# Five changes to an attention and mixture-of-adapters kernel: the first batch's patch sums on TensorE, the router on GpSimd, the up-projection moved within a slot, later batches prepared in equal steps, tail copies on ScalarE

## The chip, the cores and the metric

One core of one Trainium2 chip. The metric is device time in microseconds (us), the median of several executions of the same program; lower is better. A *span* is the length of one profiled execution inside the core, about 2 us shorter than the time that is measured around it.

TensorE (PE in the profile) multiplies matrices, PEld loads its weights, VectorE is DVE, ScalarE is ACT, GpSimd is POOL, and SyncE (SP) issues transfers. PEclk is the share of TensorE's full clock that was granted; the profile shows 1.00 where its record of the clock has not begun yet, which matters below.

## The reference, cut to what matters

```python
def _attn_ref(q, kv, w_sr):                     # q (4, 12288, 128), kv (4, 384, 32, 128)
    kv_pool = kv.reshape(B, H//4, 4, W//4, 4, C).mean(axis=(2, 4))   # 4x4 patches
    k = v = kv_pool.reshape(B, -1, C) @ w_sr                         # 768 keys per batch
    a = softmax(q @ k.T / sqrt(C))                                   # written out there
    return a @ v

def _moe_ref(x, w_gate, A, B):                  # x: 49152 tokens, 8 experts of rank 16
    logits = x @ w_gate
    # the two largest logits of each token, softmax over the two -> w
    # delta = sum over the two experts of w * ((x @ A[e]) @ B[e])
    return x + delta
```

## The kernel before: the parts that matter here

The 49152 tokens are cut into 96 chunks of 512, 24 to a batch. The main loop runs one *slot* per chunk position `k`. In slot `k` TensorE computes the scores of chunk `k` in three pieces, and ScalarE takes their exponential (`em`). TensorE also attends chunk `k-4`, and VectorE normalizes chunk `k-5`. An older chunk goes through transposes, down-projection, gate and up-projection (`tts`, `h_ps`, `hg`, `d_ps`, `osb`). Every fourth slot *routes*: it computes the expert weights of four chunks at once. The last eight chunks are routed in the smaller groups 2, 2, 2, 1, 1.

```python
    def prepare(b, adder):                      # pool, project and lay out one batch's keys and values
        ...                                     # pool_step: u += v on `adder`, five steps per third of the batch
        for h in range(3):
            for step in range(5):
                if adder is nc.vector:
                    n = w = 1024 if step < 3 else 512
                else:
                    n, w = 1024 if step < 3 else 512, 512
                ...
        def keys(h):
            ...
            for i in range(2):
                mm(ps[:, i], kvr[b, h][:, 0, 0, i, 0:C], id_f, is_transpose=True, start=(i == 0), stop=(i == 1))
            keep(nc.vector.tensor_scalar(kpT[:, 2 * h:2 * h + 2], ps, 1.0 / 16.0, None, op0=ALU.mult))
        def keys2(h): ...                       # w_sr x kpT -> kfT
        def values(h):                          # three of the six blocks each, two calls
            ...
    def route(k0, step):
        ...
        if step == 0:
            keep(nc.vector.tensor_tensor(m12, so[:, :, 0], so[:, :, 1], op=ALU.add))
            keep(nc.vector.scalar_tensor_tensor(arg, lg, 2.0, m12..., op0=ALU.mult, op1=ALU.subtract))
            keep(nc.scalar.activation(th, arg, AF.Tanh, bias=0.0, scale=0.5))
            keep(nc.vector.tensor_tensor(mask, lg, so[:, :, 1]..., op=ALU.is_ge))
        else:
            keep(nc.vector.scalar_tensor_tensor(w[:, 0:n], th, 1.0, mask, op0=ALU.add, op1=ALU.mult))   # gw
    ...
    for m in range(GC):                         # the start
        turn_q(0, m, nc.scalar)                 # 16 transposes of q on TensorE
    sums, rest = prepare(0, nc.vector)
    for h in range(3):
        for item in sums[h] + rest[2 * h:2 * h + 2]:    # VectorE adds, then keys, keys2
            item()
        for k in range(LA):
            scores(k, h)
    for item in rest[6:]:                       # values
        item()
    ...
    for k in range(LA, last + 2):               # the slots
        ...                                     # 9 <= i < 21: GpSimd adds the next batch's kv, two or three a slot
        if ks: scores(k, 0)
        if kn is not None: normalize(kn)        # rinv, xn
        for x_, h_ in pairs: transposes(x_, h_) # tt_ps, then the copy tts on VectorE
        ...
        if ks: scores(k, 1)
        if ka is not None: attend(ka, 0)
        if kn is not None:
            top(kn)                             # srt
            if ends: route(first[kn], 0)
        for h_ in kh[:1]: up(h_)                # d_ps
        if ks: scores(k, 2)
        for h_ in kh[:1]: finish(h_)            # osb and the store
        if ends: route(first[kn], 1)
        for x_ in kx[:1]:
            down(x_)
            gate(x_)                            # hg = h_ps * gw
        ...                                     # the rest of attend; one or two preparation steps from i = 18 on
```

The softmax here doesn't subtract the row's maximum and nothing guards it: scores larger than these inputs give would overflow.

## Time and profile before

| what | value | where it is read |
|---|---|---|
| time | 467.4 us median (466.7 to 469.2, 4 runs) | the times |
| span of the profiled run | 462.2 us | head of the page |
| start, to chunk 1's reciprocal | 47.46 us | timeline of VectorE |
| clean slot | 3.83 us | distance of reciprocals |
| routing slot, GpSimd quiet / adding | 0.28 / 0.5 to 3.1 us more | the same |
| preparing one later batch | about 6.9 us over eight slots | the same |
| chunk 88's reciprocal to the end | 41.0 us | the same |

Each slot has exactly one VectorE reciprocal, `rinv`, so the distance between two of them is the cost of a slot. That cuts the span into three stretches: the start (to chunk 1), the loop (chunk 1 to chunk 88, 87 slots), and the tail. I use chunk 1 and not chunk 0, because the change takes chunk 0 early.

From the page of the kernel before, the busy time of two engines, the granted clock in 40 equal slices (tenths), and the chain of work that ended last:

```profile
PE 406.1 (88%) x4475; PEld 302.1 (65%) x4547; DVE 364.9 (79%) x1033; ACT 295.6 (64%) x325; POOL 97.0 (21%) x101
...
PEclk9658999999999999999999999999999999999996
...
PE 43%; DVE 31%; issue 5%; DVEq 0%
```

TensorE is the busiest engine, but VectorE holds almost a third of the chain: both decide the time. The clock that the profile shows is low in slices 2 to 4, in the start, and in the last slice.

Groups of instructions of the kernel before (line, engine, operation, result and operands, shapes, count; then busy us and the mean ns of one; then idle time before them):

```profile
L281 DVE TENSOR_TENSOR mask<-xn,srt 128x128 f32<-128x128 f32 x22 | 13.0, 592 | 0.0
...
L275 DVE SCALAR_TENSOR_TENSOR arg<-xn,m_3051 128x128 f32<-128x128 f32 x1 | 0.3, 294 | 0.0
...
L167 POOL TENSOR_TENSOR kvr<-kvr 128x512 f32<-128x512 f32 x63 | 78.7, 1272 | 183.4 <-PE tt_ps L67 57.9 <-PE sg L67 56.6 <-DMA kvr<-in_kv_dram 44.2
```

The same `arg` takes 0.29 us in this slot and 1.30 us in another (next view), and 1.30 is about the length of one GpSimd add, 1.27 us. The timeline of the kernel before shows them side by side in one routing slot (start, length in us, engine, line, operation). The first and last line are the two reciprocals that bound the loop; VectorE and GpSimd were asked for separately:

```profile
47.46 0.18 DVE L241 RECIPROCAL rinv<-acc 128x4 f32<-128x4 f32 x1 [1.91 <-PE acc L67]
...
89.33 1.30 DVE L275 SCALAR_TENSOR_TENSOR arg<-xn,m_1165 128x128 f32<-128x128 f32 x1
90.55 0.28 DVE L281 TENSOR_TENSOR mask<-xn,srt 128x128 f32<-128x128 f32 x1
...
91.36 1.05 DVE L287 SCALAR_TENSOR_TENSOR gw<-th,mask 128x128 f32<-128x128 f32 x1
...
85.52 4.97 POOL L167 TENSOR_TENSOR kvr<-kvr 128x512 f32<-128x512 f32 x4 [0.72 <-DMA kvr<-in_kv_dram]
90.42 0.53 POOL L78 DMA_DIRECT2D qbf_1451<-in_q_dram  x1
90.96 1.28 POOL L167 TENSOR_TENSOR kvr<-kvr 128x512 f32<-128x512 f32 x1
...
421.16 0.17 DVE L241 RECIPROCAL rinv<-acc 128x4 f32<-128x4 f32 x1
```

`arg` ends at 90.63 us, just behind GpSimd's run of four adds (85.52 + 4.97 = 90.49 us); `mask`, the same size, ran right after it in 0.28 us while GpSimd issued a transfer; `gw` then stretched beside the next add.

Waits of the kernel before (engine and line, what it waited for, us in total, times, longest):

```profile
PEld L67 <- DVE tts L305: 19.1, 91, 0.8
...
DVE osb L332 <- PE d_ps L67: 14.9, 67, 0.7
```

The first is a stall of some 0.2 us in nearly every slot: the up-projection's weights wait for VectorE's copy `tts`.

Busy time in stretches of the kernel before (the first line names the columns; busy us and count of instructions per engine, then the granted clock):

```profile
core 0: us, PE busy (x) PEld busy (x) DVE busy (x) ACT busy (x) POOL busy (x), PEclk, DMA share, GB/s
...
13.00:18.00 5.00, 1.85 (x4) 0.79 (x4) 2.76 (x5) 0.00 (x0) 0.00 (x0) 0.63 1.09 381
18.00:23.00 5.00, 3.83 (x9) 0.96 (x9) 4.79 (x6) 3.59 (x4) 0.00 (x0) 0.50 1.09 380
...
33.00:38.00 5.00, 3.79 (x10) 1.69 (x11) 0.46 (x2) 3.03 (x4) 0.00 (x0) 0.50 0.87 145
38.00:43.00 5.00, 4.33 (x34) 3.29 (x33) 1.43 (x4) 3.06 (x5) 0.00 (x0) 0.98 0.88 242
```

So the start ran TensorE at half clock from about 14.3 to 38 us. From 10.3 to 15.2 us TensorE was idle, waiting for VectorE's first sums.

### The profile page before, as it was taken

The numbers are of one execution on the slowest core, as the hardware profiler recorded it, in microseconds if no ns is written. First come the engines' busy times: TensorE is split into PE (matmuls) and PEld (weight loads), VectorE is DVE, ScalarE is ACT, GpSimd is POOL, SyncE is SP. The second block draws the span as 40 slices with busy tenths as digits, with TensorE's granted clock in tenths as the row PEclk, the third lists the DMA queues.
The fourth block names the chain that finished last, engine by engine and source line by source line (L and its number), as shares of the span: only waits on it lengthen the run. The fifth ranks groups of instructions, "written<-read, shape, count | busy, mean of one in ns | idle before, by whom it ended". The sixth has DMA issues, their size and how long they took to land.

```text
span 462.2 us, 11209 instructions
## 1 busy us (share of the span) xinstructions
PE 406.1 (88%) x4475; PEld 302.1 (65%) x4547; DVE 364.9 (79%) x1033; ACT 295.6 (64%) x325; POOL 97.0 (21%) x101
## 2 busy tenths in 40 slices
PE   4578998989999988979999988978999999999872
PEld 3126776766777766756777766756677777777761
DVE  2752588878688888878788888897788888888995
ACT  3338976756577667756667777755667777777300
POOL 0011734810000835720000537450000000000000
PEclk9658999999999999999999999999999999999996
DMA  8998949985237978996145899999234244422222
GB/s 279 377 221 201 214 137 216 260 184 119 71 90 196 253 215 225 254 203 142 47 115 126 251 246 230 256 194 207 70 94 115 69 115 116 109 75 70 70 92 91
DMA packets 127427, 76.42 MB, mean 165 GB/s; under 512 B 50480, under 2 KB 126512, under 8 KB 127024
## 3 DMA queue, kind: packets, MB, share of 16 engines
q1 hardware_dynamic: 126384, 64.11, 51.6%
q0 software_dynamic: 704, 11.54, 13.4%
q8 instruction: 35, 0.57, 0.5%
q14 instruction: 16, 0.13, 0.1%
q10 hardware_dynamic: 288, 0.07, 0.1%
HBM read 50.53 MB, written 36.70 MB: 189 GB/s over the span
## 4 chain that ended last, share of the span: by engine, by line
PE 43%; DVE 31%; issue 5%; DVEq 0%
PE acc L67 17%; PE sg L67 10%; DVE xn L246 8%; DVE tts L305 7%; PE d_ps L67 5%; PE h_ps L67 4%; DVE hg L319 3%; PE tt_ps L67 3%; DVE mask L281 3%; DVE gw L287 2%; DVE srt L265 1%; DVE rinv L241 1%; PE kfT_ps L67 1%; PE v_ps L67 1%; DVE kfT L198 1%
## 5 line engine op out<-in xcount | busy, mean ns | idle before, releaser
L229 ACT ACTIVATE em<-sg 128x1024 f16<-128x1024 f32 x288 | 284.2, 1021 | 120.9 <-PE sg L67 87.2
L67 PE MATMUL acc<-vx,em 128*128 128x137 f16 x2304 | 174.9, 224 | 8.3 <-DVE xn L246 5.4
L67 PEld LDWEIGHTS <-em 128*128 128x128 f16 x2304 | 150.1, 98 | 36.6 <-DVE xn L246 30.6
L67 PE MATMUL sg<-qT,kfT 128*128 128x512 bf16 x504 | 159.7, 390 | 3.9 <-ACT em L229 1.6
L167 POOL TENSOR_TENSOR kvr<-kvr 128x512 f32<-128x512 f32 x63 | 78.7, 1272 | 183.4 <-PE tt_ps L67 57.9
L67 PEld LDWEIGHTS <-tts 128*128 128x128 bf16 x768 | 51.2, 98 | 41.3 <-DVE tts L305 19.1
L332 DVE TENSOR_TENSOR osb<-d_ps,xn 128x512 f32<-128x512 f32 x96 | 66.2, 689 | 14.9 <-PE d_ps L67 14.9
L246 DVE TENSOR_TENSOR xn<-acc,rinv 128x544 f32<-128x544 f32 x96 | 69.6, 725 | 3.4
L319 DVE TENSOR_TENSOR hg<-h_ps,gw 128x512 bf16<-128x512 f32 x96 | 66.3, 691 | 2.6
L305 DVE COPY tts<-tt_ps 128x1024 bf16<-128x1024 bf16 (+1 forms) x99 | 65.9, 670 | 0.8 <-PE tt_ps L67 0.7
L67 PEld LDWEIGHTS <-kfT 128*128 128x128 bf16 x576 | 46.8, 99 | 13.6 <-issue 8.0
L67 PEld LDWEIGHTS <-xn 128*128 128x128 bf16 x384 | 29.1, 98 | 31.3 <-issue 8.8
L67 PE MATMUL tt_ps<-id_bf,xn 128*128 128x128 bf16 x384 | 37.1, 219 | 10.1 <-DVE osb L332 6.2
L67 PE MATMUL tt_ps<-id_bf,hg 128*128 128x128 bf16 x384 | 37.3, 220 | 7.6 <-DVE hg L319 7.6
L67 PE MATMUL d_ps<-b_bf,tts 128*128 128x128 bf16 x384 | 38.5, 223 | 4.3 <-DVE tts L305 1.1
L241 DVE RECIPROCAL rinv<-acc 128x4 f32<-128x4 f32 x96 | 17.2, 179 | 30.6 <-PE acc L67 30.6
L67 PE MATMUL h_ps<-a_bf,tts 128*128 128x128 bf16 x384 | 37.1, 219 | 1.2
L265 DVE MAX8 srt<-xn 128x8 f32<-128x8 f32 x384 | 34.9, 154 | 0.1
L67 PEld LDWEIGHTS <-hg 128*128 128x128 bf16 x384 | 24.9, 98 | 9.7 <-DVE hg L319 9.7
L279 ACT ACTIVATE th<-arg 128x128 f32<-128x128 f32 (+2 forms) x27 | 8.0, 298 | 30.3 <-DVE arg L275 30.0
L167 DVE TENSOR_TENSOR kvr<-kvr 128x1024 f32<-128x1024 f32 (+1 forms) x12 | 13.1, 1090 | 6.0 <-DMA kvr<-in_kv_dram 5.4
L207 DVE CAST vx<-v_ps 128x408 f16<-128x408 f32 x8 | 4.7, 584 | 12.1 <-PE v_ps L67 12.0
(112 smaller groups left out, 129.8 us busy)
## 6 DMA issues: line engine op xcount, KB each, us to landing
kvr<-in_kv_dram SPq DMA_DIRECT2D x96, 256.0 KB, 4.8
out_dram<-osb SPq DMA_DIRECT2D x96, 256.0 KB, 2.8
qf<-in_q_dram SPq DMA_DIRECT2D x4, 256.0 KB, 5.6
qbf_286<-in_q_dram POOLq DMA_DIRECT2D x1, 512.0 KB, 5.9
qbf_288<-in_q_dram POOLq DMA_DIRECT2D x1, 512.0 KB, 7.8
qbf_507<-in_q_dram POOLq DMA_DIRECT2D x1, 512.0 KB, 9.9
qbf_810<-in_q_dram POOLq DMA_DIRECT2D x1, 512.0 KB, 7.1
qbf_1127<-in_q_dram POOLq DMA_DIRECT2D x1, 512.0 KB, 6.5
```

The lines of the kernel that those rows point to most:

```text
L67: return keep(nc.tensor.matmul(*a, **k))
L167: keep(adder.tensor_tensor(u[:, lo:hi], u[:, lo:hi], v[:, lo:hi], op=ALU.add))
L229: keep(nc.scalar.activation(em[k][:, 2 * r:2 * r + 2], ps, AF.Exp, bias=0.0, scale=scale))
L241: keep(nc.vector.reciprocal(ri, acc[k][:, :, VC]))
L246: keep(nc.vector.tensor_tensor(x, acc[k][:, :, 0:VC], ri.unsqueeze(2).broadcast_to([P, S, VC]), op=ALU.mult))
L265: keep(nc.vector.max(srt[k0][:, m, s], xn[k][:, s, C:VC]))
L279: keep(nc.scalar.activation(th, arg, AF.Tanh, bias=0.0, scale=0.5))
L281: keep(nc.vector.tensor_tensor(mask, lg, so[:, :, 1].unsqueeze(2).broadcast_to([P, n, 8]), op=ALU.is_ge))
L287: keep(nc.vector.scalar_tensor_tensor(w[:, 0:n], th, 1.0, mask, op0=ALU.add, op1=ALU.mult))
L305: keep(nc.vector.tensor_copy(sb[:, lo:hi], ps[:, lo:hi]))
L319: keep(nc.vector.tensor_tensor(hg[k].rearrange("p s (e r) -> p (s e) r", e=E), hp[k].rearrange("p s (e r) -> p (s e) r", e=E), gw[k0][:, m ...
L332: keep(nc.vector.tensor_tensor(osb, dp[k], xn[k][:, :, 0:C], op=ALU.add))
```

## The change

The intent has five parts:

1. **Start.** VectorE adds only neighbouring row pairs (four adds per third of the batch). The rest of the 4x4 sum is made by 16 accumulating transposes on TensorE, where there were 2. The values of a third come right behind its scores, and chunk 0 is attended before the first slot's scores.
2. **Router on GpSimd**, with one extra slot before the gate that uses it.
3. **`up` behind the third scores** of a slot, so that it need not wait for the copy `tts`.
4. **Preparation of later batches** in three equal steps per third, with the GpSimd adds issued later in the slot.
5. **Tail:** once no scores are left, the `tts` copies go to ScalarE.

```diff
+        def pair_step(h, r, x):
+            u, v = (kvr[b, h][:, r + i, x].rearrange("p g c -> p (g c)") for i in range(2))
+            keep(adder.tensor_tensor(u, u, v, op=ALU.add))
 ...
-            for i in range(2):
-                mm(ps[:, i], kvr[b, h][:, 0, 0, i, 0:C], id_f,
-                   is_transpose=True, start=(i == 0), stop=(i == 1))
+            if adder is nc.vector:
+                parts = [(r, x, c) for r in (0, 2) for x in range(2) for c in range(2)]
+            else:
+                parts = [(0, 0, 0)]
+            for n, (r, x, c) in enumerate(parts):
+                for i in range(2):
+                    mm(ps[:, i], kvr[b, h][:, r, x, i, c * C:(c + 1) * C], id_f, is_transpose=True,
+                       start=(n == 0 and i == 0), stop=(n == len(parts) - 1 and i == 1))
 ...                                             # values: two blocks in each of three calls
-            keep(nc.vector.tensor_tensor(m12, so[:, :, 0], so[:, :, 1], op=ALU.add))
-            keep(nc.vector.scalar_tensor_tensor(arg, lg, 2.0, m12..., op0=ALU.mult, op1=ALU.subtract))
+            def over(i):                        # lg - so[i]
+                keep(nc.gpsimd.tensor_tensor(d, lg, so[:, :, i]..., op=ALU.subtract))
+            arg, mask = over(0), over(1)
+            keep(nc.gpsimd.tensor_tensor(arg, arg, mask, op=ALU.add))
             keep(nc.scalar.activation(th, arg, AF.Tanh, bias=0.0, scale=0.5))
-            keep(nc.vector.tensor_tensor(mask, lg, so[:, :, 1]..., op=ALU.is_ge))
+            keep(nc.gpsimd.tensor_scalar(mask, mask, 0.0, None, op0=ALU.is_ge))
 ...
-            keep(nc.vector.scalar_tensor_tensor(w[:, 0:n], th, 1.0, mask, op0=ALU.add, op1=ALU.mult))
+            keep(nc.gpsimd.tensor_tensor(w[:, 0:n], th, mask, op=ALU.mult))
+            keep(nc.gpsimd.tensor_tensor(w[:, 0:n], w[:, 0:n], mask, op=ALU.add))
 ...
-        keep(nc.vector.tensor_copy(sb[:, lo:hi], ps[:, lo:hi]))
+        if tail:                                # tail = not ks: no scores left
+            keep(nc.scalar.copy(sb[:, lo:hi], ps[:, lo:hi]))
+        else:
+            keep(nc.vector.tensor_copy(sb[:, lo:hi], ps[:, lo:hi]))
 ...
-        for item in sums[h] + rest[2 * h:2 * h + 2]:
+        for item in sums[h] + rest[3 * h:3 * h + 2]:
             item()
         for k in range(LA):
             scores(k, h)
-    for item in rest[6:]:
-        item()
+            if k == 1:
+                rest[3 * h + 2]()               # values of this third
 ...
-        enter.setdefault(first[k] + size[k] + LA + (k - first[k]), []).append(k)
+        e = first[k] + size[k] + LA + (k - first[k]) + (size[k] == GC)
+        enter.setdefault(e, []).append(k)
 ...                                             # GpSimd's adds: from the head of a slot to its end
+        if k == LA:
+            for s in range(S):                  # chunk 0 attended before the scores
+                attend(ka, s)
+            ka = None
 ...
-        for h_ in kh[:1]:
-            up(h_)
         if ks:
             scores(k, 2)
         for h_ in kh[:1]:
+            up(h_)
             finish(h_)
```

More of the change, by code (lines that the diff above doesn't have):

```diff
@@ L167, in pool_step @@
             keep(adder.tensor_tensor(u[:, lo:hi], u[:, lo:hi], v[:, lo:hi], op=ALU.add))
+        def pair_step(h, r, x):
+            u, v = (kvr[b, h][:, r + i, x].rearrange("p g c -> p (g c)") for i in range(2))
+            keep(adder.tensor_tensor(u, u, v, op=ALU.add))
         for h in range(3):
-            block = []
-            for step in range(5):
-                if adder is nc.vector:
-                    n = w = 1024 if step < 3 else 512
-                else:
-                    n, w = 1024 if step < 3 else 512, 512
-                for lo in range(0, n, w):
-                    block.append(lambda h=h, step=step, lo=lo, w=w: pool_step(h, step, lo, lo + w))
-            sums.append(block)
+            if adder is nc.vector:
+                sums.append([lambda h=h, r=r, x=x: pair_step(h, r, x)
+                             for r in (0, 2) for x in range(2)])
+                continue
+            sums.append([lambda h=h, step=step, lo=lo: pool_step(h, step, lo, lo + 512)
+                         for step in range(5) for lo in range(0, 1024 if step < 3 else 512, 512)])
         st = {}
@@ L187, in keys @@
             ps = mtile([P, 2, P], name="kpT_ps")
-            for i in range(2):
-                mm(ps[:, i], kvr[b, h][:, 0, 0, i, 0:C], id_f,
-                   is_transpose=True, start=(i == 0), stop=(i == 1))
+            if adder is nc.vector:
+                parts = [(r, x, c) for r in (0, 2) for x in range(2) for c in range(2)]
[5 more added lines that the diff above has]
+                       start=(n == 0 and i == 0), stop=(n == len(parts) - 1 and i == 1))
             keep(nc.vector.tensor_scalar(kpT[:, 2 * h:2 * h + 2], ps, 1.0 / 16.0, None,
@@ L203, in values @@
                 keep(nc.vector.memset(vx[b][:, :, VC:VE], 1.0))
-            ps = mtile([P, 3, VC], name="v_ps")
-            for i in range(3):
-                mm(ps[:, i], st["kpT"][:, 3 * h + i], wext, start=(i == 0), stop=(i == 2))
-            keep(nc.vector.tensor_copy(vx[b][:, 3 * h:3 * h + 3, 0:VC], ps))
+            ps = mtile([P, 2, VC], name="v_ps")
+            for i in range(2):
+                mm(ps[:, i], st["kpT"][:, 2 * h + i], wext, start=(i == 0), stop=(i == 1))
+            keep(nc.vector.tensor_copy(vx[b][:, 2 * h:2 * h + 2, 0:VC], ps))
         for h in range(3):
-            rest.append(lambda h=h: keys(h))
-            rest.append(lambda h=h: keys2(h))
-        for h in range(2):
-            rest.append(lambda h=h: values(h))
+            for f in (keys, keys2, values):
+                rest.append(lambda h=h, f=f: f(h))
         return sums, rest
@@ L271, in route @@
         if step == 0:
-            m12 = rpool.tile([P, GC * S], FP32, tag="m12", name="m12")[:, 0:n]
-            keep(nc.vector.tensor_tensor(m12, so[:, :, 0], so[:, :, 1], op=ALU.add))
-            arg = rpool.tile([P, GC * S, 8], FP32, tag="arg", name="arg")[:, 0:n]
-            keep(nc.vector.scalar_tensor_tensor(
-                arg, lg, 2.0, m12.unsqueeze(2).broadcast_to([P, n, 8]),
-                op0=ALU.mult, op1=ALU.subtract))
+            def over(i):
+                d = rpool.tile([P, GC * S, 8], FP32, tag=f"over{i}", name=f"over{i}")[:, 0:n]
+                keep(nc.gpsimd.tensor_tensor(
+                    d, lg, so[:, :, i].unsqueeze(2).broadcast_to([P, n, 8]), op=ALU.subtract))
+                return d
+            arg, mask = over(0), over(1)
+            keep(nc.gpsimd.tensor_tensor(arg, arg, mask, op=ALU.add))
             th = rpool.tile([P, GC * S, 8], FP32, tag="th", name="th")[:, 0:n]
             keep(nc.scalar.activation(th, arg, AF.Tanh, bias=0.0, scale=0.5))
-            mask = rpool.tile([P, GC * S, 8], FP32, tag="mask", name="mask")[:, 0:n]
-            keep(nc.vector.tensor_tensor(
-                mask, lg, so[:, :, 1].unsqueeze(2).broadcast_to([P, n, 8]), op=ALU.is_ge))
+            keep(nc.gpsimd.tensor_scalar(mask, mask, 0.0, None, op0=ALU.is_ge))
             rt[k0] = th, mask
@@ L286, in route, with transposes @@
             w = rpool.tile([P, GC * S, 8], FP32, tag="gw", name="gw")
-            keep(nc.vector.scalar_tensor_tensor(w[:, 0:n], th, 1.0, mask, op0=ALU.add, op1=ALU.mult))
+            keep(nc.gpsimd.tensor_tensor(w[:, 0:n], th, mask, op=ALU.mult))
+            keep(nc.gpsimd.tensor_tensor(w[:, 0:n], w[:, 0:n], mask, op=ALU.add))
             gw[k0] = w
-    def transposes(kx, kh):
+    def transposes(kx, kh, tail):
         ps = mtile([P, 2, S, P], BF16, name="tt_ps")
@@ L347 @@
             scores(k, h)
-    for item in rest[6:]:
-        item()
+            if k == 1:
+                rest[3 * h + 2]()
+    rest = []
     late = const.tile([P, 1], FP32)
@@ L387 @@
                 load_kv(b + 1, h, j, 1)
-            if 9 <= i < 21:
-                h, j = divmod(i - 9, 4)
-                for _ in range(3 if j == 3 else 2):
-                    if sums[h]:
-                        sums[h].pop(0)()
+        if k == LA:
+            for s in range(S):
+                attend(ka, s)
+            ka = None
         if ks:
@@ L399 @@
         for x_, h_ in pairs:
-            transposes(x_, h_)
+            transposes(x_, h_, not ks)
         if k + 1 in range(GC + 1, 2 * GC):
@@ L432 @@
         kh = kx
+        if b + 1 < B and 9 <= i < 21:
+            h, j = divmod(i - 9, 4)
+            for _ in range(3 if j == 3 else 2):
+                if sums[h]:
+                    sums[h].pop(0)()
         if i >= 18 and rest:
```

## The prediction

> **What bounds it now** (span 462.2 us). The timeline, by the spacing of the `rinv` reciprocals (one a slot):
> - Clean slots take 3.83 us, TensorE almost without gaps; its regular stall, about 0.16 us, is `d_ps` waiting for the `tts` copy (waits: 19.1 us in 91 cases). VectorE has about 0.6 us free.
> - Every fourth slot routes. Quiet ones cost 0.28 us more than clean; the nine in which GpSimd adds `kvr` cost 0.5 to 3.1 us more. All routing excess, slots 8 to 92: 21.8 us. The groups show why: `mask` 592 ns on average (284 median), `m12` up to 1.45 us, `arg` up to 1.30 us, beside a 1.27 us GpSimd add. The Trainium skill, "SBUF — State Buffer", "Who interferes with whom": a VectorE instruction with two SBUF inputs contends with a GpSimd one that reads SBUF; the loser blocks for the whole instruction. The trace agrees.
> - Preparing the next batch adds 20.2 us in 15 slots (keys and keys2 together 1.75, values 1.21).
> - Start: 44 us to the first `rinv`, granted clock 0.50 from 15 to 38 us. Tail: VectorE 9.4 of 10 us busy from 440 to 450.
>
> **What changes.**
> 1. Router on GpSimd. VectorE loses about 1.0 us per group, and the blocking. Six GpSimd operations of 128x128: from 1.27 us (512 elements) and 0.73 (256) I estimate 0.45 us each. Tanh's argument comes about 1.5 us after `srt`, and tanh stands ahead of the third exp in ScalarE's queue: that exp ends 1.2 us late, the next slot loses an estimated 0.5 us. The 21.8 us become about 11: saved 11. The extra slot before gating hides `gw` for groups of four, not for the last five small groups, where `hg` will wait about 1 us each.
> 2. `up` behind the third scores: the `tts` stall goes, but the scores wait for their PSUM buffer until the first exp ends. Net 0.09 us a slot: 7 us.
> 3. Values in three pieces, fewer paired key steps: 2 us in all.
> 4. Start: per third, VectorE's 4.9 us of adds become four of 0.69 (2.8), but transposes grow from 2 to 16. At half clock 2 take 0.68 us; 16, an estimated 3.7, partly overlapped. Value copies now stand ahead of the next adds. The Trainium skill, "TensorE: Matmul & The Clock Gate", Part 4, says transposes do not count as busy for the clock gate; I expect 0.5 to stay until about 38 us. Attending chunk 0 early fills a 0.7 us wait. Net 0.5 us saved.
> 5. Tail: `tts` copies (0.67 us) leave VectorE, but ScalarE's take about 1 us. Net 1.5 us saved, the stalls of point 1 included.
>
> Sum: about 22 us off. **Predicted 446 us, 438 to 457 in 8 of 10.** Faster by over 2%: 0.88; within 2%: 0.11; slower: 0.01.
>
> **What would show it.** No routing group on VectorE, none of its groups stretched beside GpSimd; routing slots at 4.2 to 4.4 us whether GpSimd adds or not; `th` waiting for GpSimd's `over` (tens of us); clean slots near 3.75 us, the `tts` wait gone, scores waiting for `em`; preparation excess near 18 us; first `rinv` at about the same time; granted clock 0.50 in the start; in the tail, `hg` waiting for `gw`.
>
> **What would make it wrong.** GpSimd operations far slower than 0.45 us, or held behind adds that wait for data: tanh then stops ScalarE, and routing slots cost 1 us or more. Clean slots not shortened, if VectorE becomes the limit (`osb` starts later). The start: if the transposes restore the full clock, it gains about 6 us; if value copies and half-speed transposes add up, it loses 2 to 4.

## The result, and the profile after

| | before | after |
|---|---|---|
| time, median | 467.4 us (466.7 to 469.2, 4 runs) | 432.3 us (431.4 to 433.4, 4 runs) |
| span of the profiled run | 462.2 us | 431.2 us |
| to chunk 1's reciprocal | 47.5 | 42.6 |
| chunk 1 to chunk 88 | 373.7 | 345.3 |
| chunk 88 to the end | 41.0 | 43.4 |

The ratio is 0.9245, with a 95% interval of 0.9206 to 0.9283. Here and below a ratio is the mean time of one kernel's fast runs over that of the other's of the same rounds, so it is not quite the ratio of the medians quoted. All runs compared are in the fast state; one execution of the kernel before in a_router's group (470.05 us) was in the slow one and is left out.

The change is faster by 31.0 us between the profiled spans and by 35.1 us between the medians, because the profiled execution of the kernel before (464.0 us) was one of its shorter ones. I account for the 31.0 us, for which there are traces. The predicted range, 438 to 457 us, did not hold the result.

From the page of the kernel after, the same three lines:

```profile
PE 401.7 (93%) x4589; PEld 311.3 (72%) x4589; DVE 315.4 (73%) x916; ACT 293.8 (68%) x335; POOL 165.0 (38%) x263
...
PEclk9899999999999999999999999999999999999996
...
PE 78%; DVE 8%; ACT 6%; issue 2%; POOL 2%; SPq 2%; DMA 1%; POOLq 0%; ACTq 0%; DVEq 0%
```

VectorE has gone from 31% to 8% of the chain, and TensorE from 43% to 78%. The low slices of the clock in the start are nearly gone, although the prediction said they would stay.

Busy time in stretches of the kernel after, columns as before:

```profile
13.00:18.00 5.00, 3.74 (x14) 1.67 (x13) 1.24 (x4) 0.67 (x1) 0.00 (x0) 0.68 1.08 377
18.00:23.00 5.00, 4.32 (x26) 2.68 (x25) 3.27 (x6) 3.12 (x4) 0.00 (x0) 0.98 1.09 381
```

After its first rise the clock fell for 3.4 us (14.8 to 18.2 us) instead of 23.9.

Timeline of the kernel after: the bounding reciprocals, and one routing slot on GpSimd and ScalarE:

```profile
42.57 0.18 DVE L245 RECIPROCAL rinv<-acc 128x4 f32<-128x4 f32 x1 [5.14 <-PE acc L67]
...
65.57 0.42 POOL L278 TENSOR_TENSOR over_865<-xn,srt 128x128 f32<-128x128 f32 x1 [4.04 <-DVE srt L269]
...
66.46 0.46 POOL L283 TENSOR_TENSOR over_865<-over_865,over_867 128x128 f32<-128x128 f32 x1
67.01 0.52 POOL L286 TENSOR_SCALAR over_867<-over_867 128x128 f32<-128x128 f32 x1
67.62 0.46 POOL L291 TENSOR_TENSOR gw<-th,over_867 128x128 f32<-128x128 f32 x1
...
66.95 0.31 ACT L285 ACTIVATE th<-over_865 128x128 f32<-128x128 f32 x1 [0.88 <-POOL over_865 L283]
67.16 3.75 ACT L233 ACTIVATE em<-sg 128x1024 f16<-128x1024 f32 x4
...
387.85 0.18 DVE L245 RECIPROCAL rinv<-acc 128x4 f32<-128x4 f32 x1
```

GpSimd's operations take 0.42 to 0.52 us, close to the 0.45 I had estimated. Tanh (`th`) waits for them. The exponentials behind it then run at a pitch of 3.75 / 4 = 0.94 us, faster than the 1.02 us that one shows alone, so they catch up: the routing slot takes 3.94 us against 3.76 for a clean one, whether GpSimd adds or not. That is 0.18 us, where I had estimated 0.5.

Waits of the kernel after (the last line from the stretch 387 to 432 us alone):

```profile
DVE osb L340 <- PE d_ps L67: 56.0, 94, 1.9
...
POOL over_5617 L278 <- DVE srt L269: 12.2, 1, 12.2
...
DVE hg L327 <- POOL gw L292: 2.2, 3, 1.2
```

No wait of TensorE for `tts` on VectorE is listed any more; instead VectorE's `osb` waits 56.0 us for TensorE, where it waited 14.9. In the loop TensorE is now the limit, and GpSimd waits for work. The last line shows the gate waiting for the router's last step, only in the tail.

### The profile page after: what moved, and what is told of

Its sections match the earlier page's. It is cut to its first block, busy times and chain, and to the rows that moved or that the text cites. A ratio compares the mean times of both kernels' runs of the same rounds, so it can differ in the third digit from the quotient of the medians.

```text
span 431.2 us, 11431 instructions
## 1 busy us (share of the span) xinstructions
PE 401.7 (93%) x4589; PEld 311.3 (72%) x4589; DVE 315.4 (73%) x916; ACT 293.8 (68%) x335; POOL 165.0 (38%) x263
## 4 chain that ended last, share of the span: by engine, by line
PE 78%; DVE 8%; ACT 6%; issue 2%; POOL 2%; SPq 2%; DMA 1%; POOLq 0%; ACTq 0%; DVEq 0%
PE acc L67 31%; PE sg L67 26%; PE tt_ps L67 8%; PE h_ps L67 5%; PE d_ps L67 5%; ACT em L233 4%; DVE xn L250 3%; PE kfT_ps L67 2%; PE kpT_ps L67 1%; SPq L93 1%; DMA kvr<-in_kv_dram 1%; PE v_ps L67 1%; DVE vx L213 1%; ACT tts L311 1%; DVE kpT L197 1%
## 5 line engine op out<-in xcount | busy, mean ns | idle before, releaser
L233 ACT ACTIVATE em<-sg 128x1024 f16<-128x1024 f32 x288 | 274.6, 1023 | 86.3 <-PE sg L67 86.3
L67 PE MATMUL sg<-qT,kfT 128*128 128x512 bf16 x576 | 171.1, 380 | 4.7 <-ACT em L233 2.6
L67 PEld LDWEIGHTS <-em 128*128 128x128 f16 x2304 | 151.7, 98 | 30.8 <-DVE xn L250 19.7
L327 DVE TENSOR_TENSOR hg<-h_ps,gw 128x512 bf16<-128x512 f32 x96 | 65.4, 681 | 4.0 <-POOL gw L292 2.2
L67 PEld LDWEIGHTS <-kfT 128*128 128x128 bf16 x576 | 49.7, 97 | 17.6 <-issue 6.3
L313 DVE COPY tts<-tt_ps 128x1024 bf16<-128x1024 bf16 (+1 forms) x89 | 60.6, 683 | 0.0
L67 PE MATMUL tt_ps<-id_bf,xn 128*128 128x128 bf16 x384 | 37.1, 219 | 3.8 <-DVE xn L250 2.2
L67 PE MATMUL d_ps<-b_bf,tts 128*128 128x128 bf16 x384 | 37.4, 220 | 2.0 <-ACT tts L311 1.7
L67 PE MATMUL h_ps<-a_bf,tts 128*128 128x128 bf16 x384 | 37.1, 219 | 0.6 <-ACT tts L311 0.4
L245 DVE RECIPROCAL rinv<-acc 128x4 f32<-128x4 f32 x96 | 17.3, 180 | 17.8 <-PE acc L67 14.3
L311 ACT COPY tts<-tt_ps 128x1024 bf16<-128x1024 bf16 (+1 forms) x10 | 8.0, 844 | 15.4 <-PE tt_ps L67 12.8
L171 DVE TENSOR_TENSOR kvr<-kvr 128x512 f32<-128x512 f32 x12 | 7.7, 687 | 6.3 <-DMA kvr<-in_kv_dram 6.2
L213 DVE CAST vx<-v_ps 128x272 f16<-128x272 f32 x12 | 5.3, 445 | 9.1 <-PE v_ps L67 9.0
```

The costliest lines, as they stand in the source:

```text
L67: return keep(nc.tensor.matmul(*a, **k))
L171: keep(adder.tensor_tensor(u, u, v, op=ALU.add))
L213: keep(nc.vector.tensor_copy(vx[b][:, 2 * h:2 * h + 2, 0:VC], ps))
L233: keep(nc.scalar.activation(em[k][:, 2 * r:2 * r + 2], ps, AF.Exp, bias=0.0, scale=scale))
L245: keep(nc.vector.reciprocal(ri, acc[k][:, :, VC]))
L311: keep(nc.scalar.copy(sb[:, lo:hi], ps[:, lo:hi]))
```

## The experiments

The questions were two. First: why did the start gain 4.9 us, where I predicted 0.5? Theory T says that the transposes count as activity and hold TensorE's clock. Its rival V says that transposes do not count (so the Trainium skill, "TensorE: Matmul & The Clock Gate", Part 4) and that the value matmuls, now early, restore it. Second: where do the other 26 us come from, above all the routing? The rivals are that GpSimd's adds block VectorE's router operations, or that VectorE just had too much work. Kernels of one group below shared a chip and the runs of the kernel before (its median was 465.9 to 466.8 us in the four groups).

All kernels that ran, cut by the same three stretches of their traces (us):

| kernel | to chunk 1 | chunk 1 to 88 | to the end | span | time, median (ratio to before) |
|---|---|---|---|---|---|
| before | 47.46 | 373.70 | 41.0 | 462.2 | 467.4 |
| a_sums | 44.57 | 374.56 | 41.1 | 460.2 | 462.8 (0.989) |
| a_values | 53.54 | 373.13 | 41.0 | 467.7 | 470.1 (1.007) |
| a_start | 41.22 | 380.71 | 41.1 | 463.0 | 463.3 (0.990) |
| warm_tr | 44.87 | 374.62 | 41.0 | 460.5 | 463.8 (0.995) |
| warm_mm | 48.54 | 374.26 | 41.0 | 463.8 | 465.3 (0.999) |
| a_router | 46.73 | 353.35 | 44.8 | 444.9 | 446.9 (0.958) |
| r_start | 41.19 | 353.39 | 44.8 | 439.4 | 441.4 (0.950) |
| u_up | 43.01 | 350.67 | 43.3 | 437.0 | 438.1 (0.938) |
| u_tail | 41.64 | 345.30 | 46.1 | 433.0 | 436.3 (0.934) |
| after | 42.57 | 345.28 | 43.4 | 431.2 | 432.3 (0.925) |
| t_route | 41.44 | 345.26 | 42.3 | 429.0 | 431.7 (0.926) |
| t_both | 44.02 | 345.12 | 43.2 | 432.3 | 432.1 (0.927) |
| pairs | 43.50 | 342.40 | 43.4 | 429.3 | 430.7 (0.924) |
| late_tanh | 41.70 | 341.60 | 43.3 | 426.6 | 428.4 (0.920) |
| best | 41.28 | 338.84 | 43.0 | 423.1 | 424.9 (0.912) |
| best2 | 40.99 | 338.90 | 42.1 | 422.0 | 424.0 (0.911) |

### a_sums, a_values, a_start: the start, in parts

To the kernel before were added the pair sums with accumulating transposes (a_sums), the values in three parts behind the scores (a_values), or both (a_start). The diffs are those of the change; the short one is a_values:

```diff
-            ps = mtile([P, 3, VC], name="v_ps")
+            m = 2 if b == 0 else 3
+            ps = mtile([P, m, VC], name="v_ps")
 ...
-    for item in rest[6:]:
-        item()
+            if k == 1:                          # inside the loop over scores(k, h)
+                rest[6 + h]()
```

> The kernel before with one part of the change alone: the first batch's patches summed by 4 half-size VectorE adds and 16 accumulating transposes per third; value projections stay at the end of the start. After the change the granted clock came back at 18 us, before it at 38 us. Theory V (the value matmuls placed between the scores make TensorE busy enough, transposes do not count): the clock stays at 0.50 from about 15 to 38 us, and at half clock 16 transposes cost more than VectorE saves, so the second reciprocal (chunk 1; 47.5 us before, 42.6 after the change) comes at about 49 to 50 us, total 1 to 3 us slower. Theory T (the transposes restore the clock): full clock from about 20 us, chunk 1's reciprocal at 42 to 44 us, total 4 to 5 us faster.

> The kernel before with the other part alone: the first batch's value projections in three pieces of two, each behind the second chunk's scores of its third; the sums stay on VectorE as before. Theory V: full clock from about 21 us, since value matmuls fill the wait for ScalarE; but VectorE now copies the values ahead of its 4.9 us of adds, so no time is gained: chunk 1's reciprocal at about 49 to 50 us, total 1 to 3 us slower. Theory T: clock at 0.50 until about 38 us, chunk 1's reciprocal at 51 us or later.

> The kernel before with both parts of the start, nothing else of the change. Both theories: full clock from about 18 to 19 us, chunk 1's reciprocal at about 43 us (4 to 5 us earlier than before), total 4 to 5 us faster, ratio about 0.990. If it gains less than 2 us, the start of the changed kernel owes its 4.9 us to attending chunk 0 ahead of the scores.

Measured: a_sums 462.8 us, ratio 0.989 (0.983 to 0.996), with half clock only from 15.6 to 22.4 us, and chunk 1 came 2.9 us earlier: near what T expected, far from V. a_values 470.1 us, ratio 1.007 (1.002 to 1.013), chunk 1 6.1 us later (53.5 us, where V expected 49 to 50 and T 51 or later). The clock fell three times, from 13.2 to 23.5, from 26.9 to 33.7, and from 37.1 to 43.9 us. It came back each time behind a stretch of scores and value matmuls, without a transpose (TensorE busy 3.13 of 3.3 us from 20.1, 3.30 from 30.3 and 2.95 from 40.6 us), and was lost again in the next wait for VectorE's sums. So this half of V is supported: the early values, by filling the waits between the scores, help to restore the clock, though alone they gain nothing. (Scores alone can do it too where they leave few gaps: in a_router the clock came back at 30.2 us behind scores that kept TensorE busy 3.14 of the 3.4 us before.) In a_start the clock, once up at 10.9 us, stayed at 1.00 through the rest of the start and chunk 1 came 6.2 us earlier, but the time was only 463.3 us, ratio 0.990 (0.983 to 0.997).

Where did a_start's 6.2 us go? Its loop took 380.7 us instead of 373.7, and slot 8 alone took 8.01 us (4.36 before). Slots 9 and 17 lost another 0.9 and 1.5 us; in them the clock was at half, from 55.3 to 58.7 and from 92.8 to 96.2 us. The timeline of a_start in that slot, VectorE and then GpSimd:

```profile
49.38 1.32 DVE L284 TENSOR_TENSOR m<-srt 128x16 f32<-128x16 f32 x1
50.74 1.30 DVE L286 SCALAR_TENSOR_TENSOR arg<-xn,m 128x128 f32<-128x128 f32 x1
51.96 1.35 DVE L292 TENSOR_TENSOR mask<-xn,srt 128x128 f32<-128x128 f32 x1
53.41 1.67 DVE L298 SCALAR_TENSOR_TENSOR gw<-th,mask 128x128 f32<-128x128 f32 x1
...
46.94 6.22 POOL L167 TENSOR_TENSOR kvr<-kvr 128x512 f32<-128x512 f32 x5
...
53.65 1.27 POOL L167 TENSOR_TENSOR kvr<-kvr 128x512 f32<-128x512 f32 x1
```

All four router operations met an add, one after the other, and each was as long as one: the earlier start had moved the slot under GpSimd's adds. So the two parts of the change lean on each other; r_start, below, tests that.

### b_noadds: the adds taken away, with a wrong result

```diff
                     if sums[h]:
-                        sums[h].pop(0)()
+                        sums[h].pop(0)
```

> The kernel before without GpSimd's adds of the next batch's patches (wrong result on purpose: only one of 16 patches enters the keys of batches 1 to 3). Theory of blocking (router operations with two SBUF inputs blocked by GpSimd's adds): mask, m12 and arg fall to 0.28, 0.19 and 0.29 us everywhere, the nine loaded routing slots from 0.5 to 3.1 us over a clean slot to about 0.28 us, and the total by about 15 us (ratio about 0.967). Rival (the routing slots cost what VectorE's own router work takes): the slots stay and the total changes by less than 3 us.

The result is wrong as intended (relative error 0.86), and the time is 483.6 us, ratio 1.035: slower, against the sum that was expected. The trace shows both sides. Every routing slot after the first took 4.11 us, 0.28 more than a clean one, as in the quiet slots before: no add, no stretching. But one slot took 37.03 us, 33.2 over a clean one. Waits of b_noadds, TensorE's and then SyncE's own:

```profile
PE sg L67 <- DMA qT<-qbf: 32.1, 1, 32.1
...
SPq L83 <- DMA qbf<-in_q_dram: 48.2, 1, 48.2
```

With nothing to add, GpSimd issued its casting transfers of q one behind the other, every 2.5 us until 65.7 us, and the transposed load that TensorE needed was held until 82.3 us. That the adds had also paced the transfers is argued from this order, not tested. Without that one stall the span would be 480.7 - 33.2 = 447.5 us against 462.2, an estimate from this trace. The run confirms the blocking slot by slot (except in slot 8, which had the stall), but its total time shows nothing about it. The nine loaded routing slots of the kernel before lie 14.8 us above 4.11 us in all.

### a_router: only the router on GpSimd, with its extra slot

The diff is the router's part of the change and the `(size[k] == GC)` of `enter`.

> The kernel before with the router on GpSimd and the extra slot before gating, nothing else. If the routing slots are as in the changed kernel (0.18 us over a clean slot whether GpSimd adds or not), the routing excess falls from 21.8 to about 4 us: 16 to 18 us faster, ratio about 0.963, clean slots still at 3.83 us. My prediction's 0.5 us per routing slot would give 11 us. The tail gets about 1 us longer, hg waiting for gw of the small groups.

446.9 us, ratio 0.958 (0.952 to 0.963). The loop fell from 373.70 to 353.35 us, by 20.35 us, with the old start and everything else as before. Routing slots took 3.83 us, exactly as long as clean ones. The tail got longer, from 41.0 to 44.8 us. The load removed from VectorE is about 1.0 us in each of some 22 groups when nothing blocks, and quiet routing slots cost 0.28 us more than clean ones, 22 x 0.28 = 6 us; the rest of the 20 us is what blocking had cost. The 14.8 us from b_noadds agree. So most of this is blocking and a smaller part is load.

### r_start: a_router and both parts of the new start

> The kernel before, with both parts of the new start (sums by accumulating transposes, values behind each third's scores) and the router on GpSimd with its extra slot; up-projection, later batches' order and the tail as before. If the start alone gained little only because GpSimd's adds blocked the router (slot 8 took 8.0 us there): slots 8 and 9 below 4.2 us, chunk 1's reciprocal at 41 to 44 us, and the time about 440 to 442 us, that is 5 to 6 below the router alone (446.9). If the start's gain is given back whatever routes: about 444 to 447 us, with a longer slot somewhere after the start.

441.4 us, ratio 0.950 (0.947 to 0.953). Chunk 1 came at 41.19 us, as in a_start, slots 8 and 9 took 3.31 and 3.66 us, and the loop took 353.39 us, as in a_router. With the router on GpSimd the start's gain arrives in full: 46.73 - 41.19 = 5.5 us, and the span fell by 5.5 us too. The first expectation held; that the gain is given back whatever routes fell.

Four of the six executions took 441.2 to 441.4 us at a mean clock of 0.988 to 0.990, and two took 444.6 us (0.975) and 444.9 us (0.978). The clock still falls in some executions; where it fell in these two was not traced.

### warm_tr and warm_mm: transposes against ordinary matmuls in the gap

To the kernel before, 28 useless operations in TensorE's idle time from 10.3 us on, as transposes or as ordinary matmuls of the same operands:

```diff
     for m in range(GC):
         turn_q(0, m, nc.scalar)
+    for n in range(7):
+        idle = mtile([P, S, P], name="idle")
+        for i in range(S):
+            mm(idle[:, i], id_f, id_f, is_transpose=True, start=(i == 0), stop=(i == S - 1))
```

(warm_mm has the same without `is_transpose=True`; its trace shows two records for each, 56.)

> The kernel before, with 28 fp32 transposes of the identity into unused PSUM tiles (about 4 us of them, from about 10.3 us on), in TensorE's idle gap between the q transposes and the first batch's keys. If transposes count for the clock gate: the granted clock stays 1.00 past 14 to 15 us, where it fell to 0.50 in the kernel before, and falls, if it does, only some 3.5 to 5 us after the added ones have ended, so not before about 18 us. If they do not count, as the skill says: it falls at 13.6 to 14.8 us as before, or earlier. Time within 2% of before under both; the first reciprocal moves by less than 4 us.

> Control: the same 28, as ordinary fp32 matmuls (each longer than a transpose). The granted clock stays 1.00 past 15 us under both theories, and falls later than 18 us if at all. If this run drops at 14 us too, the idea of filling the gap is wrong and the pair says nothing. Time within 2% of before.

Timeline of warm_tr, TensorE (the multiplication that makes the gate's weights, the transposes of q, the added ones, and the first ordinary matmuls after them):

```profile
3.64 0.60 PE L67 MATMUL w_ps<-w_gate_sb,wT 128*128 128x8 f32 x2 [0.38 <-DVE wT L145]
6.70 3.76 PE L67 MATMUL qT_ps<-id_f,qf 128*128 128x128 f32 x16 [2.47 <-DMA qf<-in_q_dram]
10.28 4.33 PE L67 MATMUL idle<-id_f 128*128 128x128 f32 x28
...
16.43 0.70 PE L67 MATMUL kfT_ps<-kpT,w_sr_sb 128*128 128x256 f32 x2 [0.52 <-DVE kpT L191]
```

The added transposes alone in two stretches of equal length (TensorE busy and its weight loads, then the clock as shown):

```profile
10.55:12.25 1.70, 1.70 (x9) 1.56 (x9) 1.00 1.03 351
12.60:14.30 1.70, 1.70 (x18) 1.70 (x17) 1.00 1.07 368
```

Stretches of warm_tr:

```profile
13.00:18.00 5.00, 2.85 (x20) 2.08 (x20) 3.59 (x6) 0.00 (x0) 0.00 (x0) 1.00 1.09 379
18.00:23.00 5.00, 2.37 (x9) 0.69 (x7) 4.29 (x5) 3.77 (x4) 0.00 (x0) 0.97 1.09 382
23.00:28.00 5.00, 3.73 (x8) 1.33 (x9) 3.60 (x5) 1.70 (x2) 1.09 (x2) 0.50 0.88 237
```

Stretches of warm_mm:

```profile
18.00:23.00 5.00, 2.69 (x9) 0.99 (x10) 4.14 (x5) 2.71 (x3) 0.00 (x0) 1.00 1.09 381
23.00:28.00 5.00, 2.48 (x8) 0.97 (x9) 3.52 (x7) 1.28 (x3) 0.59 (x2) 0.80 0.87 231
```

In warm_tr TensorE did nothing but transposes from 4.2 to 16.4 us. The two stretches of equal length hold 9 transposes and then 18, one in 0.21 us and then one in 0.11: the clock doubled between them. The record of the clock begins there, at 12.5 us, with full clock; the 1.00 that the profile shows before only means that nothing was recorded. So transposes alone raised the clock, as they did in the other traces: in 17 of the 18 (all but the control) TensorE ran nothing but transposes in the 3.4 us before the record begins with full clock, and the q transposes before it ran at one in 0.21 us.

The transposes also held the clock past 14.3 us, where it fell in the kernel before; that it lasted to about 22.7 us is also the work of the ordinary matmuls from 16.4 us on. The control with ordinary matmuls doubled its pace at about 12.3 us, ended its added work 3.1 us later (17.7 instead of 14.6 us) and lost the clock 3.2 us later, at about 26.0. Transposes raised and held the clock like ordinary matmuls, so T is shown, and the statement that they do not count is contradicted. What the pair does not exclude is the other half of V, that the early values help as well (a_values). As a side effect, chunk 1 came 2.6 us earlier in warm_tr, although it does useless work: time 463.8 us, ratio 0.995 (0.990 to 0.999); in warm_mm it came 1.1 us later, 465.3 us, ratio 0.999 (0.996 to 1.002).

### u_up and u_tail: the change with one part taken back

```diff
 # u_up: up before the third scores again
+        for h_ in kh[:1]:
+            up(h_)
         if ks:
             scores(k, 2)
         for h_ in kh[:1]:
-            up(h_)
             finish(h_)
 # u_tail: tail copies on VectorE again
-            transposes(x_, h_, not ks)
+            transposes(x_, h_, False)
```

> The changed kernel with the up-projection put back ahead of the third scores. Theory (the copy's stall of 0.16 us returns and the scores' wait for their buffer goes): clean slots 3.83 instead of 3.76 us, about 5 to 6 us slower than the changed kernel (ratio to before about 0.937). Rival (the shorter slot comes from VectorE having less to do): clean slots stay at 3.76 us, no change.

> The changed kernel with the tail's tts copies back on VectorE. From chunk 92's reciprocal to the end it took 43.4 us after the change, 41.0 before. Intent of the change (VectorE is the limit in the tail): 3 us or more slower. Theory (latency is the limit: a ScalarE copy of 128x1024 takes 1.0 us against 0.69, and up and down wait for it): 1 to 2 us faster than the changed kernel.

u_up took 438.1 us, ratio 0.938 (0.934 to 0.943). Its loop took 350.67 us, against 345.28 in the change: moving `up` is worth 5.4 us in the loop. Clean slots went back from 3.76 to 3.83 us, but routing slots to 3.83 as well, from 3.94. So the late tanh costs time only once `up` has moved and the slot has become short enough.

u_tail took 436.3 us, ratio 0.934 (0.929 to 0.939). Its tail took 46.1 us instead of 43.4. I had suspected the slower ScalarE copies of lengthening the tail; that fell. But not all of the 2.7 us is the copies' work. One slot of u_tail's tail, from 415.7 to 421.6 us, took 5.8 us (4.7 in r_start, whose tail copies are on VectorE too), and most of it ran at half clock:

```profile
417.10:420.40 3.30, 3.30 (x33) 3.30 (x31) 2.06 (x8) 0.23 (x1) 1.50 (x6) 0.50 0.18 50
```

Without that slot's 1.2 us the copies on ScalarE save some 1.5 us, an estimate from these two traces. Whether copies on VectorE make the clock fall there more often was not tested; the mean clock of u_tail's executions was 0.978 to 0.989, that of the change's 0.987 to 0.992.

### t_route and t_both: the small groups of the tail routed on VectorE

In t_route the groups smaller than four take the old VectorE code; t_both takes the tail copies back to VectorE as well.

```diff
-        if step == 0:
+        if size[k0] < GC:
+            route_dve(k0, step, n, lg, so)      # the old VectorE router
+        elif step == 0:
```

> The changed kernel with the last five small groups routed on VectorE as before; no GpSimd adds run there. Theory (hg waits for gw through GpSimd, ScalarE and GpSimd, 2.2 us in all in the tail): 1 to 2 us faster than the changed kernel, hg waiting for nothing. Rival (VectorE is the limit in the tail): no change or slower by about 1 us.

> The changed kernel with both tail undoings: tts copies on VectorE and the five small groups routed on VectorE. If latency is the limit in the tail: 2 to 3 us faster than the changed kernel, chunk 92's reciprocal to the end about 41 us as before the change. If VectorE is the limit: slower by 2 us or more.

t_route: tail 42.3 us, 1.1 less than in the change; time 431.7 us, ratio 0.926 (0.921 to 0.930), not distinguishable from the change by time. t_both: tail 43.2 us, no gain, time 432.1 us. With the adds long over in the tail, VectorE's router is not blocked, and the small groups do not wait for GpSimd; the price is VectorE's time, which the ScalarE copies leave free. Of the tail's excess over the kernel before I can place 1.1 us this way; 1.3 us remain, and I did not find out what they are.

### late_tanh and pairs: two steps on from the change

late_tanh issues tanh in the gating part of the slot, behind the third exponential. pairs does two preparation steps in every second slot.

```diff
 # late_tanh
-            th = rpool.tile([P, GC * S, 8], FP32, tag="th", name="th")[:, 0:n]
-            keep(nc.scalar.activation(th, arg, AF.Tanh, bias=0.0, scale=0.5))
 ...
-            rt[k0] = th, mask
+            rt[k0] = arg, mask
         else:
-            th, mask = rt.pop(k0)
+            arg, mask = rt.pop(k0)
+            th = rpool.tile([P, GC * S, 8], FP32, tag="th", name="th")[:, 0:n]
+            keep(nc.scalar.activation(th, arg, AF.Tanh, bias=0.0, scale=0.5))
 # pairs
-            if len(rest) > NB - 1 - i:
+            if i % 2:
```

> The changed kernel with tanh issued on ScalarE behind the third exp of the routing slot instead of ahead of it. Theory (the 0.18 us that a routing slot still costs is the third exp held behind a tanh that waits for GpSimd): routing slots become clean slots of 3.76 us, 22 x 0.18 = 4 us faster than the changed kernel, ratio to before about 0.915. Rival (the 0.18 us has another cause): no change. In the small groups of the tail hg may wait longer, up to 1 us in all.

> The changed kernel with the preparation of a batch laid out as one slot of keys and one of keys2 with values, three times over, so that keys and keys2 never share a slot. In the changed kernel keys with keys2 cost 1.78 us over a clean slot, keys 0.38, keys2 with values about 0.9 without routing. Theory (a slot with both keys steps pays for TensorE, VectorE, TensorE, VectorE in a row): a batch costs 3 x (0.38 + 0.9) = 3.8 us instead of 5.3, three batches 4 us faster, ratio to before about 0.915. Rival (the cost is the sum of the work wherever it stands): no change.

late_tanh: 428.4 us, ratio 0.920 (0.916 to 0.925); routing slots took 3.76 us, exactly a clean slot, and the loop fell from 345.28 to 341.60 us. ScalarE in late_tanh, in the slot shown for the change:

```profile
63.14 2.85 ACT L233 ACTIVATE em<-sg 128x1024 f16<-128x1024 f32 x3 [0.91 <-PE sg L67]
65.96 0.31 ACT L289 ACTIVATE th<-over 128x128 f32<-128x128 f32 x1
```

Tanh follows the third exponential without any wait. pairs: 430.7 us, ratio 0.924 (0.919 to 0.928), by time not distinguishable from the change; the loop took 342.40 us, 2.9 less than the change, where 4 had been expected.

### best and best2: the parts that helped, together

best is the change with late_tanh, pairs and t_both. best2 has the tail copies on ScalarE again except in the last two slots:

```diff
-            transposes(x_, h_, not ks)
+            transposes(x_, h_, not ks and k < last)
```

> Late tanh, the paired preparation and both tail undoings together. If the three add up: 4 + 4 + 2.5 us faster than the changed kernel, about 421 us, ratio to before about 0.90.

> The changed kernel with tanh moved to the gating slot, two preparation steps in every second slot, small groups routed on VectorE, and the tail's copies on ScalarE except in the last two slots, where VectorE has room. From the earlier best (424.9) and the copies' worth of 2 to 3 us in the tail: 421 to 424 us; last chunk's group to the end below 43.0 us. If the copies on ScalarE are worth nothing once VectorE routes: 424 to 426.

best 424.9 us, ratio 0.912 (0.908 to 0.916); 421 had been expected, so the parts did not add up in full. best2 424.0 us, ratio 0.911 (0.909 to 0.913); its tail is 0.9 us shorter in the trace (42.1 against 43.0), but the times of the two cannot be told apart. Both beat the change by about 8 us.

## Why the prediction was wrong

The signs of four of its five terms were right, and so was the mechanism that I put first, but the sum was 9 us short. The stretches of a_router, u_up, r_start and late_tanh allow each term to be measured. The tanh that is late on GpSimd is counted with the router, as in the prediction (345.28 - 341.60 = 3.7 us). That is a choice of account: in a_router the late tanh cost nothing yet, and in the order in which the runs add the parts the router is worth 20.35 us and `up` 5.4.

| term | predicted | measured | from |
|---|---|---|---|
| 1 router, loop | 11 | 20.35 - 3.7 = 16.7 | before to a_router, less late_tanh's gain |
| 2 `up` | 7 | 5.4 + 3.7 = 9.1 | u_up to late_tanh |
| 3 preparation | 2 | 2.7 | r_start to u_up, loop |
| 4 start | 0.5 | 4.9 | before to after, chunk 1 |
| 5 tail, with the router's stalls | 1.5 | -2.3 | before to after |
| sum | 22 | 31.0 | |

- **Point 4, "I expect 0.5 to stay until about 38 us", failed as a mechanism.** It rested on the Trainium skill, "TensorE: Matmul & The Clock Gate", Part 4, that transposes do not count as busy. warm_tr shows that they do: with nothing but transposes since 4.2 us the clock rose from half to full at about 12.5 us. The trace of before had already held the evidence. From 4.3 to 10.3 us TensorE ran only the q transposes, at one in 0.21 us, and full clock is recorded from 10.9 us on. It fell at about 14.3 us, after 3.4 us in which TensorE ran nothing, the idle window that Part 1 of the same page names. In the changed kernel the first third's 16 transposes run in that gap; the clock fell at 14.8 us all the same, but was back at 18.2. Before that return TensorE ran no transpose, only key projections, scores and the first value matmuls (busy 2.78 of 3.3 us from 14.9 us on); a_sums, without early values, had to wait until 22.4 us. So the prediction missed two things: that transposes count, and that early values fill the waits. The start gained 4.9 us in the profiled pair and 5.5 in r_start against a_router. The prediction's own alternative, "if the transposes restore the full clock, it gains about 6 us", was the right one.
- **How much of the start's gain is the clock, and how much luck.** Nine traces have the changed kernel's start (after, u_up, u_tail, t_route, t_both, pairs, late_tanh, best, best2). Chunk 1 came at 41.0 to 41.7 us in the five in which the clock, once up, did not fall, at 42.6 and 43.0 in the two with 3.4 us at half clock, and at 43.5 and 44.0 in the two with 6.8 us. warm_tr, with the old start and 6.8 us at half clock, reached it at 44.9. So, as an estimate from these traces, about 1 us of the 4.9 is the shorter adds and the rest the clock. Whether the clock fell differed between executions of the same start, so the pair could as well have shown 3.4 or 6.5 us. Attending chunk 0 early was not run alone; a_start and r_start do without it and came to chunk 1 at 41.2 us, so no gain of it shows.
- **Point 1 was right in its mechanism and mis-sized.** The blocking by GpSimd's adds is shown: without adds the routing slots took 4.11 us each (b_noadds), and with the router off VectorE 3.83 (a_router). The term that was off is "the next slot loses an estimated 0.5 us". Measured, it is 0.18 us; the exponentials behind tanh ran at a pitch of 0.94 us and used up the 0.91 us that ScalarE otherwise waits for scores in a slot. Over some 20 slots that is 3.7 us, where I had let the late tanh cost 11.
- **Point 2 was right in its size, and in half of its mechanism.** Predicted were clean slots near 3.75 us; measured 3.76. The wait for `tts` went, and `osb` waits for `d_ps`, which starts later. That the scores would wait for `em` in its place does not show: 1.6 us in all before, 2.6 after, and 2.7 in u_up. What takes back part of the `tts` stall stays open. Its 2 us more came in the preparation slots: those (27 slots, nine a batch) fell from 122.4 to 117.6 us in the loop between u_up and late_tanh, which the prediction had not counted for `up`.
- **Point 3 was right**, 2.7 against 2 us. That the whole preparation excess fell from about 6.9 to 5.3 us a batch is in part point 2's doing.
- **Point 5 failed in sign.** The router on GpSimd made the tail 3.8 us longer (a_router); the ScalarE copies gave back some 1.4 us (44.8 in r_start to 43.4; u_tail against after shows 2.7, of which 1.2 is the slot at half clock). I had put the two together as a gain of 1.5 us. Moving `up` cost nothing there: u_up, which differs from the change in `up` alone, has a tail of 43.3 us. `hg` does wait for `gw` in the tail, as predicted, but only 2.2 us in total; the router's path there is longer by more than this one wait shows.

Why the median fell by 4 us more than the spans is only argued. Before's executions spread over 7 us in these rounds (463 to 470 us), and a_start shows that the blocking depends on how the slots happen to lie against GpSimd's adds. In the changed kernel the routing slots outside the preparation took 3.93 to 3.95 us everywhere. No trace of one of before's longer executions was taken.

## What to carry to other kernels

Look at an operation's length slot by slot, not at its mean: the same instruction at 0.29 and 1.30 us, with the long one ending as another engine's instruction ends, is blocking, and moving it to the other engine can pay even at half the speed. A gain upstream may be eaten by such a collision (a_start), so try it again after the collision is gone (r_start) before dropping it. And where a prediction rests on a general statement about the hardware, look for a place in the trace at hand that could contradict it; here there was one. Read the clock from TensorE's own pace, too: the profile shows full clock where nothing was recorded.

## What the Trainium skill lacked or had wrong

- "TensorE: Matmul & The Clock Gate", Part 4, says that transposes do not count as busy for the clock gate. warm_tr contradicts it for fp32 transposes: with only these from 4.2 to 16.4 us, their pace doubled at about 12.5 us (9, then 18 in 1.70 us), and the clock fell at about 22.7 us, against 14.3 us without the added ones. bf16 transposes, for which the page gives its times, were not tested alone.
- The same page, Part 1, has the full clock back after about 3.4 us of sustained work. In the kernel before TensorE was busy 3.83 of 5 us from 18 to 23 us and 3.79 of 5 us from 33 to 38 us, and the clock stayed at 0.50 until about 38 us. How busy TensorE has to be is not stated. The traces narrow it: every recorded stretch of one clock but the last is a multiple of 3.41 us, and cut into such steps (18 traces), the clock never rose after a step with under 2.73 us busy and always after one with 2.94 us or more; it always fell after a step with under 1.52 us and never after one with more than 1.84 us. Between these it did both. The ends of matmuls are modelled in the profile, so the limits are estimates from these traces.
- "SBUF — State Buffer", "Who interferes with whom", agrees with the traces. What it lacks is the chain: four short VectorE operations in a row each met one of GpSimd's back-to-back adds and took 1.32, 1.30, 1.35 and 1.67 us (a_start).
- "GPSIMD Engine Reference", § 3.1, gives about 2.6 cycles per element for a two-input operation but no figure for the fixed cost of a short one. Here 128, 256 and 512 elements per partition took 0.46, 0.73 and 1.27 us: about 2.1 ns per element, and by the same line some 0.19 us fixed.
